# Scheduling constants of a four-layer attention kernel: second layer's row statistics on ScalarE, VectorE's share of the exponentials by every second pass, twelve query exponentials at a time

## The chip, the cores and the metric

The kernel runs on one core of one Trainium2 chip. The time is that of one execution in device microseconds, as a median of several runs; lower is better.

## The reference

A residual stream `x` of 2048 rows and 1024 columns (bf16) goes through two kinds of blocks, A, B, A, B, with the same two sets of weights each time:

```python
def layernorm(x): return (x - mean(x)) / sqrt(var(x) + 1e-5)

def A(x):      # 32 heads of 32: linear attention with a softmax feature map
    q, k, v = heads(x @ A_wqkv)
    pq, pk = q @ w_phi, k @ w_phi                     # per head
    phi_q = concat(softmax(pq), softmax(-pq))
    phi_k = concat(softmax(pk), softmax(-pk))
    o = (phi_q @ (phi_k.T @ v)) / (phi_q @ sum(phi_k) + 1e-6)
    return merge(o) @ A_wo

def B(x):      # 32 heads of 32: softmax attention
    q, k, v = heads(x @ B_wqkv)
    return merge(softmax(q @ k.T / sqrt(32)) @ v) @ B_wo

x = x + A(layernorm(x)); x = x + B(layernorm(x))
x = x + A(layernorm(x)); x = x + B(layernorm(x))
```

Each B block has 32 x 2048 x 2048 exponentials, and these are the bulk of the work.

## The kernel before

**Stages.** The text calls one A block with the B block after it a layer; there are two. Rows are worked in four chunks of 512, each of four row tiles of 128. A layer begins with A's keys and values (`a_keys`, line 768), then for each chunk come A's queries (`a_queries`, 927), its output projection into the residual `xR` (`a_out`, 1004, with the additions of line 1015), the layer normalisation of the result (`ln_rows`, 593) and B's first keys, queries and values (`b_k`, `b_q`, `b_v`, with evacuations at lines 1040 and 1041). Then comes B's attention (`attention`, 1171). While it runs, TensorE also computes the keys, values and queries of the other head groups, output projections (`b_out`, 1096) and, in the first layer, most of the next layer's A keys. Their results go through PSUM bank 7, which VectorE empties.

**The attention.** It is cut into 4096 units over both layers: a unit is the scores of one head for 128 keys and 512 queries, one PSUM bank. `group` (1215) collects up to three units, TensorE computes their scores (line 1197) into three adjacent banks, and ScalarE takes the exponentials of all three in one instruction (line 1257): a pass. Two sets of three banks, 0 to 2 and 3 to 5, are used in turn, so a pass can have its scores computed only when the pass two before it has been read. TensorE then multiplies by the values and by ones (line 1386) into bank 6, which VectorE copies out (line 1402); the denominators go through DRAM and come back spread over the rows.

VectorE takes some of the units: it reads one bank of scores (line 1339), and for two such units at a time computes the exponential with bit operations and a polynomial (`exp_dve`, lines 1147 to 1163). Its unit is chosen some units ahead of the pass at hand (`spare`, 1303; `AHEAD` units ahead). There are two ways for it. If bank 7 is free, the extra unit's scores go there (`attach`, 1346). If bank 7 was taken in the pass before, the pass may instead be made of two units for ScalarE, with the third bank of its set given to VectorE (lines 1236 to 1242):

```python
if make is after and w == WIDE and state["miss"] and n > state["mixed"] + mix(turn):
    third = spare({0, 1, 2, 3} - {u[4] for u in grp[:2]}, turn, [])
```

Here `n` counts passes, and `mix(turn)` from `MIX` says how many passes must lie between two such passes. `MOST` bounds the units that VectorE takes in a turn (one head group for one query chunk), `LOAD` the work that VectorE may have in hand when a new pair is begun, `NEAR` the distance at which a half-filled pair is closed, and `LEAD` how early its operations are due.

**Row statistics.** `ln_rows` has two ways to get the mean and variance of a row tile. With `dve` true, VectorE runs two `bn_stats` of 512 columns and a `bn_aggr` (lines 607 and 610). With it false, ScalarE makes two passes over the 1024 columns with a sum each, a copy and a square (613 and 615, each followed by a read of the accumulator), and VectorE forms the variance with two tiny operations (617 and 619). Then ScalarE takes a logarithm and an exponential (625, 628), and VectorE scales the rows (634). For chunks 0 to 2 of a B block the rows are stored to DRAM and read back transposed; for chunk 3 TensorE transposes them (644) and ScalarE copies them out (647), tile by tile. Line 1537 calls it with `LN_DVE[layer]`.

**The order of the work.** All instructions are first collected as operations with a planned duration, their dependencies, their buffers and a due time (`prio`). `Sched.run` (196) then plays the operations through and writes out one fixed order for each engine; the chip runs that order. An operation may start in the plan only when its buffers can be had: `QUOTA` bounds how many of each class are live (`eq` are the query exponentials of `a_queries`, `E` the attention's exponentials, `E1` those of VectorE, `xo` the normalised rows, `bc`, `mm`, `cmp`, `pk` and others the PSUM banks of A). The due times come from the constants in the diff: `KS`, `VS` and `VH` space keys and values of the second attention, `QL` is how early queries are due, `GAPS` and `GO` space the output projections, `PH` the steps of a chunk in A, `LA`, `LR`, `WO`, `KD`, `AW` and `BO` are leads or due times, and `SOON` and `WINDOW` bound how far ahead of the front a load may go. Where TensorE would have too little to do, the planner adds filler matmuls (1632, 1637, and idle calls of line 571 with `onesD`).

Of the kernel before, what the change touches and what calls it, by code (L numbers as in the profile page):

```python
# [60 lines left out]
class Sched:  # L61
# [52 lines left out]
    def _alloc(self, bufs):  # L114
# [19 lines left out]
        for b in new:  # L134
# [6 lines left out]
            else:  # L141
                room = sum(n for _, n in self.free)
                if b.cls in MODEST and room < b.size + RESERVE:
                    room = 0
# [51 lines left out]
    def run(self):  # L196
# [28 lines left out]
        while left:  # L225
            moved = False
            for e in engines:
# [6 lines left out]
                while ready[e] and len(skipped) < 400:  # L234
# [6 lines left out]
                    if item[3].bulk and self.wire > t + BACKLOG and self.live.get("S", 0):  # L241
                        skipped.append(item)
                        continue
                    if item[1] <= todo[front] + (SOON.get(item[3].bufs[0].cls, WINDOW) if e == "SP" and item[3].bufs and self.live.get("S", 0) else WINDOW) and not (
                            e == "PE" and self.wants is not None and item[3].bufs and item[3].bufs[0].cls == "fil"
# [99 lines left out]
SBUF_ARENA = 162 * 1024  # L345
WIDE = 3
WINDOW = 80.0
SOON = {"slabk": 24.0, "wo": 17.0, "w2": 5.0}
RESERVE = 10 * 1024
LONG = {"kT", "v", "slab", "slabk", "xn", "xn1", "kvacc", "kvm", "zm", "wnat"}  # L350
MODEST = {"slabk", "xn1", "e1", "vp1", "pkf", "wo", "bo"}
QUOTA = {"qf": 2, "qg": 6, "wqk": 1, "tl": 7, "pk": 4, "pv": 4, "kv": 4, "mm": 5, "cmp": 5, "bc": 6, "num": 1, "wt": 4, "wx": 2, "fil": 3,
         "e": 6, "vp": 6, "e1": 4, "vp1": 4, "E": 9, "q2": 2, "kt": 3, "w2": 5, "oT": 25, "T": 4, "den": 2,
         "eq": 8, "ns": 4, "cw": 6, "hl": 6, "oc": 2, "slab": 8, "slabk": 3, "fin": 4,
         "rs": 8, "pkf": 1, "cden": 2, "part": 8, "w2r": 1,
         "wo": 1, "st": 4, "xo": 9, "bn": 4, "xs": 1, "xy": 5, "xx": 1, "E1": 8}
CORE = {"E", "E1", "T", "den", "cden", "oT"}
E_SIZE = 3 * 1024
HOLES = 3
# [20 lines left out]
EACH = (False, False)  # L380
LAG = 6
KL = (17, 32)
KS = (3, 5.5)
VS = (5.0, 7.25)
WQ_AFTER = 2
BY_DVE = 2
LR = 13
LAG_X = 7
LN_DVE = (False, True)
LN_PE = (3, 3)  # L390
WO = 8
KD = 8
HALF = (False, True)
VH = 3.0
QL = (11, 12)
AW = 28
OUT_AT = (232, 256, 272)
GO = 3.0
BO = 295
PT = 2.5  # L400
QB = 18
PH = (1, 22, 44)
LA = 8
AHEAD_AT = 5
P0 = (133, 171, 244)
GAPS = (1.5, 1.5, 1.75)
PK = (142, 184, 260)
STEP = 2.5
AWAY = (-10, 12)
MIX = (lambda i: 2, lambda i: 2)  # L410
LOAD = (3.0, 2.5)
AHEAD = (36, 36)
SLACK = 11.0
NEAR = (26, 24)
LEAD = 3.0
MOST = (lambda i: 0 if i < 1 else 17, lambda i: 0 if i < 1 else 6 if i < 7 else 40)


def act_us(n):
# [15 lines left out]
def kernel(  # L435
# [81 lines left out]

    sch = Sched(ARENA, QUOTA)
    op = sch.op
# [63 lines left out]
    def load_x():  # L583
        for c in range(NC):
            for t in range(TB):
                after = row_done[4 * c + t - LAG_X:4 * c + t - LAG_X + 1] if c > 1 else ()
                xdone[c][t] = [dma(-21.0 if c == 0 else 10 * c - LR - 8, lambda c=c, t=t: nc.sync.dma_start(
                    out=xR[:, 4 * c + t, :], in_=A_x[0, c * C512 + t * P:c * C512 + (t + 1) * P, :]), after, kb=256)]
# [322 lines left out]
    def q_ahead(c, prio, xn):  # L911
        xb, xv, fin = xn
        for hf in range(2):
            at = prio + QA[hf]
            wb, ww, wd = slab("slabk", at - WO, wdq_v[:, :, hf * C512:(hf + 1) * C512], C512, [store["q"][hf]])
            for a in range(4):
# [254 lines left out]
    def attention(base, kT, vT, q_of, gate, most, mix, turns, pos, split, ahead, near, load, each):  # L1171
# [111 lines left out]
        def wants(prio):  # L1283
# [7 lines left out]
            if state["pair"] is None and (state["turn"].get(turn, 0) + 2 > most(turn)  # L1291
                                          or sch.live.get("xy", 0) >= QUOTA["xy"] or sch.live.get("E1", 0) >= QUOTA["E1"]):
                return False
# [186 lines left out]
    for layer in range(2):  # L1480
# [18 lines left out]
        for c in chunks:  # L1499
            if layer == 0:  # L1500
                next(rows_in)
                xnA[c] = ln_rows(c, 0, base + 10 * c - LR if c else -16.0, c < BY_DVE, c == 0, c == 0)
            else:
# [26 lines left out]
        for c in range(NC):  # L1530
# [3 lines left out]
            for hf in range(2):  # L1534
                a_queries(c, hf, pr + PH[0] * hf, wq_s, state, oc)
            a_out(c, pr + PH[1], wo_s, oc)
            xnB[c] = ln_rows(c, 1 + 2 * layer, pr + PH[1] + 1, LN_DVE[layer], c >= LN_PE[layer], c >= LN_PE[layer])
            b_k(0, c, pr + PH[2], wk0, kT, ANY, "ACT")
            if c == 0:
                q_of[(0, 0)] = b_q(0, 0, pr + PH[2] + 0.5, wq0, ANY)  # L1540
            for t in range(TB):
# [4 lines left out]
        for g in range(1, G):  # L1546
            pr = at + 10 * pos[(0, g)] - KL[layer]
            w = slab("w2", pr - 1, B_w[:, :, D + g * P:D + (g + 1) * P], P)
            for c in range(NC):
                b_k(g, c, pr + KS[layer] * c, w, kT, FIL, "DVE")  # L1550
        for c in range(NC):
            for t in range(TB):
                b_v(1, c, t, at + VS[layer] * (4 * c + t) + 2, bv_s[1], vT, FIL, "DVE")
                if HALF[layer]:
                    b_v(0, c, t, at + VH * (4 * c + t) + 3, bv_s[0], vT, FIL, "DVE", (1,))
        for g in range(G):
            pr = at + 10 * pos[(0, g)]
            w = slab("w2", pr - (QL[layer] + 3), B_w[:, :, g * P:(g + 1) * P], P) if g else wq0
            for qc in range(NC):
                if qc < side:  # L1560
                    if qc or g:
                        pq = at + 10 * pos[(qc, g)]
                        wq = w if pq < pr + 30 else slab("w2", pq - (QL[layer] + 3), B_w[:, :, g * P:(g + 1) * P], P)
                        q_of[(qc, g)] = b_q(g, qc, pq - QL[layer], wq, FIL)
                else:
                    away = q_away(g, qc, pr + (AW if last else AWAY[qc - 2]), w, FIL)
                    q_of[(qc, g)] = q_back(g, qc, at + 10 * pos[(qc, g)] - QB, away)
        oTs = attention(at, kT, vT, q_of, gate, MOST[layer], MIX[layer], turns, pos, SPLIT[layer], AHEAD[layer], NEAR[layer], LOAD[layer], EACH[layer])
        if last:
            bo_s = [slab("bo", at + BO + fc, B_o[:, :, fc * C512:(fc + 1) * C512], C512) for fc in range(2)]  # L1570
        new = [[[] for _ in range(TB)] for _ in range(NC)]
        for qc, p0, gap in ((0, P0[0], GAPS[0]), (1, P0[1], GAPS[1]), (2, P0[2], GAPS[2])):
            if last:
                p0, gap = OUT_AT[qc], GO
            for i in range(8):
                t, fc = (i // 2, i % 2) if last else (i % 4, i // 4)
                if not last and t == 0:
                    w = slab("wo", at + p0 + gap * i - WO, B_o[:, :, fc * C512:(fc + 1) * C512], C512)
                add = b_out(t, fc, qc, at + p0 + gap * i, bo_s[fc] if last else w, oTs[qc], FIL, last)
# [9 lines left out]
        for i in range(G):  # L1589
            pr = p0 - 7 + PT * i  # L1590
            t, fc = (i // 2, i % 2) if last else (i % 4, i // 4)
            if not last and t == 0:
                w = slab("wo", pr - WO, B_o[:, :, fc * C512:(fc + 1) * C512], C512)
            parts.append(b_out(t, fc, qc, pr, bo_s[fc] if last else w, oTs[qc], FIL, last, None, 0, 3))
# [15 lines left out]
        if not last:  # L1610

            kv = new_kv()
            for c, p0 in ((0, PK[0]), (1, PK[1]), (2, PK[2])):
                xb, xv, fin = xnA[c] = ln_rows(c, 2, at + p0, True, False, False, "xn1")
                w = [(wk_slab(at + p0 + KD + 14 * fc, fc, "slabk"), wv_slab(at + p0 + KD + 0.5 + 14 * fc, fc, cls="slabk")) for fc in range(2)]
                a_keys(c, at + p0 + KD, [w[0][0], w[1][0]], [w[0][1], w[1][1]], kv, FIL, True, STEP)
                xnA[c] = [dma(at + p0 + KD + 2, lambda c=c, xv=xv, i=i: nc.sync.dma_start(
                    out=xd_v[:, c, 2 * i:2 * i + 2, :], in_=xv()[:, 2 * i:2 * i + 2, :]), flat([fin]), [xb], kb=256, bulk=True)
# [54 lines left out]
```

## Time and profile before

| | us |
|---|---|
| median of 3 runs | 2249.85 (2249.02 to 2250.31) |
| the profiled execution | 2248.66 |
| its span, first to last instruction | 2246.9 |
| mean granted TensorE clock | 0.998 of full speed |

| part of the span | from | to |
|---|---|---|
| up to the first exponential pass | 0 | 331.83 |
| first attention | 331.83 | 1207.70 |
| between the attentions | 1207.70 | 1401.19 |
| second attention | 1401.19 | 2235.55 |
| after its last pass | 2235.55 | 2246.90 |

The profile lists for each group of instructions its line, engine and operation, the shapes, the count, busy time, the mean duration in ns, and the idle time of the engine just before them with what ended it. PE is TensorE, PEld its weight loads, DVE VectorE, ACT ScalarE, POOL GpSimd, SP SyncE. Consecutive instructions of an engine overlap in the records, so the durations of a row can add up to more than its busy time.

### The profile page before, as it was taken

How to read it: one execution, taken by the hardware profiler on the slowest of the kernel's cores; microseconds unless marked ns; L12 is line 12 of the kernel's file. 1: busy time of each engine (PE TensorE's matmuls, PEld its weight loads, DVE VectorE, ACT ScalarE, POOL GpSimd, SP SyncE). 2: the span in 40 equal slices, each digit the busy share in tenths (PEclk: the TensorE clock that was granted, in tenths of full speed). 3: DMA queues.
4: the chain of work that ended last, by engine and by line, in shares of the span. 5: the costliest groups of instructions: out<-in, count | busy, mean ns of one | idle time of the engine just before them, and what ended most of it. 6: DMA issues, size and time to landing. Idle time of an engine off the chain costs nothing.

```text
span 2246.9 us, 64847 instructions
## 1 busy us (share of the span) xinstructions
PE 2178.1 (97%) x28034; PEld 820.9 (37%) x28034; DVE 1856.5 (83%) x2630; ACT 1993.1 (89%) x1969; POOL 29.6 (1%) x78
## 2 busy tenths in 40 slices
PE   9999999999999999999999999999999999999999
PEld 5543443333333333333334444433333333333333
DVE  8866535998888999999998877376889997899997
ACT  7347669999999999999998444999999999999998
POOL 1000000000000000000000000000000000000000
PEclk9999999999999999999999999999999999999999
DMA  7821221112223423422546023111111111121111
GB/s 222 168 55 34 75 57 28 40 45 48 65 77 89 117 66 101 124 77 78 143 123 205 1 64 90 30 29 33 38 35 44 41 38 33 35 75 47 46 41 35
DMA packets 239672, 156.84 MB, mean 70 GB/s; under 512 B 131992, under 2 KB 213912, under 8 KB 239384
## 3 DMA queue, kind: packets, MB, share of 16 engines
q1 hardware_dynamic: 239384, 152.69, 25.1%
q8 instruction: 219, 3.59, 0.7%
q14 instruction: 69, 0.57, 0.1%
HBM read 85.79 MB, written 29.87 MB: 51 GB/s over the span
## 4 chain that ended last, share of the span: by engine, by line
PE 43%; ACT 41%; issue 8%; DVE 5%; DMA 2%; SPq 0%; ACTq 0%; DVEq 0%
ACT arena L1257 39%; PE psum L567 16%; PE psum L571 10%; PE psum L1386 7%; PE psum L1197 6%; PE psum L978 1%; ACT arena L788 1%; DVE work L1147 1%; PE psum L823 1%; DVE arena L1000 0%; DVE xR L1015 0%; PE psum L1632 0%; DVE arena L801 0%; PE psum L903 0%; DVE work L1339 0%
## 5 line engine op out<-in xcount | busy, mean ns | idle before, releaser
L1257 ACT ACTIVATE arena<-psum 128x1536 bf16<-128x1536 f32 (+1 forms) x1332 | 1671.7, 1433 | 9.0 <-PE psum L1197 5.2
L1386 PE MATMUL psum<-arena 128*32 128x512 bf16 x4322 | 657.6, 383 | 2.0 <-DVE arena L1402 1.4
L1386 PE MATMUL psum<-arena,ones_bf 128*32 128x512 bf16 x4322 | 657.8, 383 | 0.0
L571 PE MATMUL psum<-arena 128*32 128x512 bf16 (+1 forms) x9024 | 621.9, 376 | 6.4 <-DVE arena L801 1.5
L1197 PE MATMUL psum<-arena 32*128 32x512 bf16 x4096 | 522.3, 383 | 49.4 <-ACT arena L1257 42.6
L567 PE MATMUL psum<-arena 128*128 128x512 bf16 (+1 forms) x1968 | 434.6, 372 | 0.5
L1197 PEld LDWEIGHTS <-arena 32*128 32x128 bf16 x4096 | 154.3, 91 | 580.6 <-issue 573.0
L1339 DVE TENSOR_SCALAR work<-psum 128x512 int32<-128x512 f32 x405 | 277.3, 686 | 100.7 <-PE psum L1197 96.9
L1147 DVE SCALAR_TENSOR_TENSOR work<-work 128x1024 f32<-128x1024 f32 (+1 forms) x298 | 355.7, 1194 | 3.2
L571 PEld LDWEIGHTS <-arena 128*32 128x32 bf16 x9024 | 203.6, 95 | 256.5 <-issue 139.6
L1386 PEld LDWEIGHTS <-arena 128*32 128x32 bf16 x4322 | 186.0, 95 | 237.8 <-issue 156.4
L567 PEld LDWEIGHTS <-arena 128*128 128x128 bf16 x1968 | 185.7, 98 | 215.6 <-issue 17.6
L1147 DVE SCALAR_TENSOR_TENSOR arena<-work 128x1024 bf16<-128x1024 f32 (+1 forms) x206 | 246.4, 1196 | 2.5
L1386 PEld LDWEIGHTS <-ones_bf 128*32 128x32 bf16 x4322 | 184.4, 95 | 24.1 <-issue 4.0
L1041 DVE CAST arena<-psum 128x512 bf16<-128x512 f32 (+1 forms) x104 | 67.1, 645 | 64.3 <-PE psum L571 63.5
L788 ACT ACTIVATE arena<-psum 128x512 bf16<-128x512 f32 x80 | 43.7, 595 | 72.1 <-PE psum L567 65.9
L1402 DVE COPY arena<-psum 128x512 f32<-128x512 f32 x126 | 86.0, 682 | 6.3 <-PE psum L1386 5.0
L792 DVE TENSOR_REDUCE arena<-arena 128x32 f32<-128x1024 bf16 x64 | 77.7, 1214 | 16.1 <-ACT arena L788 15.7
L940 ACT ACTIVATE arena<-psum 128x512 bf16<-128x512 f32 x112 | 61.4, 604 | 25.8 <-PE psum L567 23.9
L801 DVE TENSOR_TENSOR arena<-psum,arena 128x1024 bf16<-128x1024 f32 x64 | 77.7, 1214 | 4.1 <-DVE arena L795 0.4
L1151 DVE TENSOR_SCALAR work<-work 128x1024 int32<-128x1024 int32 x114 | 77.6, 681 | 2.2
L1154 DVE TENSOR_SCALAR arena<-work 128x1024 uint16<-128x1024 uint16 x114 | 77.4, 679 | 0.0
(102 smaller groups left out, 1270.4 us busy)
## 6 DMA issues: line engine op xcount, KB each, us to landing
arena<-rd SPq DMA_DIRECT2D x62, 256.0 KB
arena<-in_B_wqkv_dram SPq DMA_DIRECT2D x51, 256.0 KB
xa<-arena SPq DMA_DIRECT2D x48, 256.0 KB
arena<-in_A_wqkv_dram SPq DMA_DIRECT2D x40, 256.0 KB
arena<-in_B_wo_dram SPq DMA_DIRECT2D x40, 256.0 KB
arena<-arena SPq DMA_DIRECT2D x256, 32.0 KB
arena<-wd_k SPq DMA_DIRECT2D x32, 256.0 KB
arena<-arena SPq DMA_DIRECT2D x62, 128.0 KB
```

Source lines behind the costliest of these rows:

```text
L567: nc.tensor.matmul(out_, lhsT=lhsT, rhs=rhs, start=start, stop=stop, skip_group_check=True)
L571: nc.tensor.matmul(out_[ks, :], lhsT=lhsT[:, ks], rhs=rhs, start=start, stop=stop, tile_position=(0, 32 * k), skip_group_check=True)
L792: red = op("DVE", dve_us(1024), lambda ev=ev, sv=sv: nc.vector.reduce_sum(out=sv(), in_=ev().rearrange("p s (h d) -> p (s h) d", d=DH), ax ...
L801: ml = op("DVE", dve_us(1024), lambda vpv=vpv, wv_=wv_, sv=sv: nc.vector.tensor_tensor(out=wv_()[:, :, :, 0:DH], in0=vpv().rearrange("p (h ...
L1147: return sch.later("DVE", dve_us(w * 512) + us, lambda: nc.vector.scalar_tensor_tensor(out=out_(), in0=in0(), scalar=scalar, in1=in1(), op ...
L1151: m = ts(lambda y_v=y_v, x_v=x_v: nc.vector.tensor_scalar(out=x_v().bitcast(I32), in0=y_v().bitcast(I32), scalar1=0x007FFFFF, scalar2=0x3F ...
L1154: a = ts(lambda y_v=y_v, e2_v=e2_v: nc.vector.tensor_scalar(out=e2_v().bitcast(U16), in0=high(y_v()), scalar1=0x7F80, scalar2=EXP2S_D, op0 ...
L1197: nc.tensor.matmul(out=out_, lhsT=kT[g][1]()[r, pp, d * P:(d + 1) * P], rhs=q_of[(qc, g)][1]()[r, (pp + j // 2) % 2, :], start=True, stop= ...
L1257: ex = make("ACT", act_us(w * C512), lambda: nc.scalar.activation(out=e_v()[:, 0:w * C512], in_=s_v()[:, 0:w * C512], func=ACT.Exp, scale= ...
L1339: pair["got"].append(sch.later("DVE", dve_us(512) + 0.13, lambda: nc.vector.tensor_scalar(out=y_v().bitcast(I32)[:, k, :], in0=s_v(), scal ...
L1386: nc.tensor.matmul(out=a_v()[col:col + 32, :], lhsT=v_v()[:, kc % 4, o:o + DH] if what == 0 else ones_bf[:], rhs=ev()[:, x * C512:(x + 1) ...
L1402: cp = op("DVE", dve_us(512), lambda t_v=t_v, a_v=a_v: nc.vector.tensor_copy(out=t_v(), in_=a_v()), [last], [a_b, t_b], prio - 4)
```

## The change

Only constants change. The second entry of `LN_DVE` becomes false; `MIX` goes from 2 to 1 in both layers; `eq` from 8 to 12; besides these some pool sizes, due times and the bounds on VectorE's share. What is computed stays the same.

```diff
-SOON = {"slabk": 24.0, "wo": 17.0, "w2": 5.0}
-RESERVE = 10 * 1024
+SOON = {"slabk": 24.0, "wo": 17.0, "w2": 6.0}
+RESERVE = 8 * 1024
-QUOTA = {"qf": 2, "qg": 6, "wqk": 1, "tl": 7, "pk": 4, "pv": 4, "kv": 4, "mm": 5, "cmp": 5, "bc": 6, "num": 1, "wt": 4, "wx": 2, "fil": 3,
-         "e": 6, "vp": 6, "e1": 4, "vp1": 4, "E": 9, "q2": 2, "kt": 3, "w2": 5, "oT": 25, "T": 4, "den": 2,
-         "eq": 8, "ns": 4, "cw": 6, "hl": 6, "oc": 2, "slab": 8, "slabk": 3, "fin": 4,
+QUOTA = {"qf": 2, "qg": 6, "wqk": 1, "tl": 7, "pk": 6, "pv": 4, "kv": 3, "mm": 6, "cmp": 3, "bc": 10, "num": 1, "wt": 4, "wx": 2, "fil": 5,
+         "e": 6, "vp": 6, "e1": 4, "vp1": 4, "E": 10, "q2": 2, "kt": 4, "w2": 5, "oT": 26, "T": 4, "den": 2,
+         "eq": 12, "ns": 4, "cw": 6, "hl": 6, "oc": 2, "slab": 8, "slabk": 3, "fin": 4,
          "rs": 8, "pkf": 1, "cden": 2, "part": 8, "w2r": 1,
-         "wo": 1, "st": 4, "xo": 9, "bn": 4, "xs": 1, "xy": 5, "xx": 1, "E1": 8}
+         "wo": 1, "st": 4, "xo": 10, "bn": 4, "xs": 1, "xy": 7, "xx": 1, "E1": 11}
...
-KS = (3, 5.5)
-VS = (5.0, 7.25)
+KS = (3, 6.5)
+VS = (5.0, 6.75)
...
-LR = 13
+LR = 12
 LAG_X = 7
-LN_DVE = (False, True)
+LN_DVE = (False, False)
 LN_PE = (3, 3)
-WO = 8
-KD = 8
+WO = 7
+KD = 9
 HALF = (False, True)
-VH = 3.0
-QL = (11, 12)
-AW = 28
+VH = 3.5
+QL = (11, 9)
+AW = 26
 OUT_AT = (232, 256, 272)
-GO = 3.0
-BO = 295
+GO = 2.6
+BO = 285
...
-PH = (1, 22, 44)
-LA = 8
+PH = (1, 22, 43)
+LA = 4
...
-GAPS = (1.5, 1.5, 1.75)
+GAPS = (1.5, 1.5, 2.75)
...
-MIX = (lambda i: 2, lambda i: 2)
-LOAD = (3.0, 2.5)
-AHEAD = (36, 36)
-SLACK = 11.0
-NEAR = (26, 24)
-LEAD = 3.0
-MOST = (lambda i: 0 if i < 1 else 17, lambda i: 0 if i < 1 else 6 if i < 7 else 40)
+MIX = (lambda i: 1, lambda i: 1)
+LOAD = (4.0, 3.5)
+AHEAD = (36, 42)
+SLACK = 12.0
+NEAR = (22, 24)
+LEAD = 2.0
+MOST = (lambda i: 0 if i < 1 else 15, lambda i: 0 if i < 1 else 6 if i < 7 else 40)
```

## The prediction

> **What bounds the kernel now.** I read the page's busy shares first, then the busy times of five stretches cut at the first and last exponential pass of each attention (line 1257), then that line by itself.
>
> ```profile
> span 2246.9 us, 64847 instructions
> PE 2178.1 (97%) x28034; PEld 820.9 (37%) x28034; DVE 1856.5 (83%) x2630; ACT 1993.1 (89%) x1969; POOL 29.6 (1%) x78
> PE 43%; ACT 41%; issue 8%; DVE 5%; DMA 2%; SPq 0%; ACTq 0%; DVEq 0%
> ```
>
> ```profile
> 0.00:331.83 331.83, 325.20 (x2794) 155.91 (x2795) 223.78 (x388) 197.16 (x374) 14.37 (x45) 0.99 0.41 103
> 331.83:1207.70 875.87, 840.12 (x12574) 292.34 (x12573) 785.07 (x1030) 868.91 (x729) 12.66 (x25) 1.00 0.29 83
> 1207.70:1401.19 193.49, 192.61 (x1386) 85.25 (x1386) 152.56 (x266) 97.72 (x196) 2.59 (x8) 1.00 0.30 84
> 1401.19:2235.55 834.36, 810.91 (x11239) 283.66 (x11238) 689.22 (x936) 827.86 (x670) 0.00 (x0) 1.00 0.15 39
> 2235.55:2246.90 11.35, 9.24 (x47) 3.74 (x44) 5.83 (x11) 1.48 (x5) 0.00 (x0) 1.00 0.28 94
> ```
>
> Columns of the stretches: length, then busy time of TensorE, its weight loads, VectorE, ScalarE and GpSimd, then the granted clock, the DMA share and GB/s. Over the whole span TensorE looks like the bound, but the stretches differ. In the two attentions ScalarE is busy 868.91 of 875.87 us and 827.86 of 834.36: idle only 7.0 and 6.5 us. Between them it is busy 97.72 of 193.49 us, and TensorE 192.61. So the attentions last as long as ScalarE's passes, and the stage between them as long as TensorE's matmuls.
>
> The Trainium skill ("Perfetto Trace Analysis", Identifying the Most-Contended Engine) says that a matmul busy share is no good measure, and the weight-load share is; the loads are 292.34 of 875.87 us here, which agrees. Read with TensorE as the bound, the first attention would go by its 32 added matmuls of the step below, in fours: some 1.8 us longer.
>
> ```profile
> 331.83:1207.70 875.87, 848.55 (x674) 1.00 0.29 83
> 1401.19:2235.55 834.36, 823.07 (x658) 1.00 0.15 39
> L1257 ACT ACTIVATE arena<-psum 128x1536 bf16<-128x1536 f32 x1027 | 1441.6, 1529 | 9.0 <-PE psum L1197 5.2 <-PE psum L571 1.5 <-PE psum L1386 1.0
> L1257 ACT ACTIVATE arena<-psum 128x1024 bf16<-128x1024 f32 x305 | 338.4, 1110 | 0.0
> 1411.83 18.91 ACT L1257 ACTIVATE arena<-psum 128x1536 bf16<-128x1536 f32 x14
> ```
>
> The first two rows are line 1257 alone in the attentions. A third bank adds 1529 - 1110 = 419 ns to a pass. The 1332 passes hold 3 x 1027 + 2 x 305 = 3691 banks, so of their 848.55 + 823.07 = 1671.6 us each pass has a fixed part of (1671.6 - 3691 x 0.419)/1332 = 0.094 us. In the last row, 14 three-bank passes run without a break: less the last one's 1.53, 13 steps of 1.335. If all passes ran so (two banks: 1.335 - 0.419 = 0.916), the first attention's 521 and 153 would take 835.7 us and the second's 506 and 152 814.7. With the other ScalarE work in them (868.91 - 848.55 = 20.4 and 4.8), 19.8 and 14.9 us are left: 34.7 us are lost to late scores, 0.026 a pass. That is the pool from which any better order can win.
>
> **The passes themselves.** The instruction order of the changed kernel has 1012 three-bank passes, 326 of two and two of one: 1340 for 3690 banks. VectorE takes 406 banks where it took 405. So "a third bank every second pass" changes when VectorE takes them, not how many. First attention: 674 to 677 passes, 1869 to 1866 banks: 3 x 0.094 - 3 x 0.419 = -0.98 us. Second: 658 to 663 passes, 1822 to 1824 banks: 5 x 0.094 + 2 x 0.419 = +1.31. Eight more passes at 0.026 of lateness: +0.2.
>
> The Trainium skill ("VectorE: DVE Perf Modes", the section on the TRN2 errata) gives ScalarE a fixed 172 cycles at 1.2 GHz for a read of PSUM, and so speaks against narrower passes: 0.143 us each, by estimate 0.4 us more over the eight. The rows give 0.094, which I take.
>
> **The row statistics.** Sixteen rows (four chunks of line 600's loop) go from two statistics and an aggregate on VectorE to two passes with a read of the sum on ScalarE, and two tiny VectorE subtractions.
>
> ```profile
> L607 DVE BATCH_NORM_STATS2 arena<-xR 128x6 f32<-128x512 bf16 x80 | 51.0, 675 | 1.2 <-DMA xR<-in_A_x_dram 1.2
> L610 DVE BATCH_NORM_AGGREGATE arena<-arena 128x2 f32<-128x12 f32 x40 | 8.2, 205 | 0.8
> L613 ACT ACTIVATE arena<-xR 128x1024 bf16<-128x1024 bf16 x24 | 25.3, 1056 | 23.1 <-DVE xR L1015 21.6 <-DMA xR<-in_A_x_dram 1.0 <-DVE arena L619 0.5
> L613 ACT ACTIVATION_READ_ACCUMULATOR arena<-xR 128x1 f32 x24 | 4.6, 190 | 0.0
> L619 DVE TENSOR_TENSOR arena<-arena 128x1 f32<-128x1 f32 x24 | 3.8, 158 | 6.5 <-ACT arena L615 5.6
> 240.00:330.00 90.00, 89.62 (x465) 39.47 (x462) 38.87 (x83) 57.44 (x109) 0.00 (x0) 1.00 0.31 78
> ```
>
> VectorE sheds 32 x 0.675 + 16 x 0.205 - 32 x 0.158 = 19.8 us, ScalarE gets 32 x (1.056 + 0.190) = 39.9. All lie between the attentions, where ScalarE would then be busy 138 of 193 us and TensorE still ends last. Cover for chunks 0 to 2: their rows leave by DMA and come back transposed, and the keys that read them stand some 20 planned microseconds later behind the next chunk's queries. The first layer already has it so, and in the last row, its stage with those chunks, TensorE is busy 89.62 of 90 us. Without cover, the 24 longer passes of those chunks would stand in front of query exponentials at 1.06 each, 25 us; I take 0. SyncE's queue has the same 1314 transfers in both orders; the 12 row stores start a microsecond or so later and keep their place ahead of their transposes.
>
> Chunk 3 has no such distance: its rows are transposed on TensorE and the keys follow at once.
>
> ```profile
> 1397.22 1.06 PE L644 MATMUL psum<-ident,arena 128*128 128x128 bf16 x16
> 1401.92 0.62 PE L644 MATMUL psum<-ident,arena 128*128 128x128 bf16 x8 [0.16 <-DVE arena L634]
> 1402.38 0.59 PE L1632 MATMUL psum<-xR,onesD 128*128 128x512 bf16 x2
> 1403.68 0.81 PE L1632 MATMUL psum<-xR,onesD 128*128 128x512 bf16 x3
> 1404.33 7.13 PE L567 MATMUL psum<-arena 128*128 128x256 bf16 x56
> 1411.39 0.60 PE L1197 MATMUL psum<-arena 32*128 32x512 bf16 x6
> ...
> 1397.42 0.69 DVE L1015 TENSOR_TENSOR xR<-xR,psum 128x512 bf16<-128x512 bf16 x1 [0.19 <-PE psum L567]
> ...
> 1397.87 2.99 ACT L647 COPY arena<-psum 128x1024 bf16<-128x1024 bf16 x3
> 1402.58 1.01 ACT L647 COPY arena<-psum 128x1024 bf16<-128x1024 bf16 x1
> 1408.00 0.58 ACT L1040 CAST arena<-psum 128x512 bf16<-128x512 f32 x1 [1.35 <-PE psum L567]
> 1411.49 0.37 ACT L1040 CAST arena<-psum 128x256 bf16<-128x256 f32 x1 [0.50 <-PE psum L567]
> ```
>
> The second layer before: the last row's sum is in xR at 1397.42 + 0.69 = 1398.11, its transposes (L644 x8) start at 1401.92, 3.81 us later, its copy (L647) ends at 1403.59. The same place in the first layer, with ScalarE's sums:
>
> ```profile
> 312.29 0.69 DVE L1015 TENSOR_TENSOR xR<-xR,psum 128x512 bf16<-128x512 bf16 x1 [0.21 <-PE psum L567]
> 319.91 0.61 PE L644 MATMUL psum<-ident,arena 128*128 128x128 bf16 x8
> ```
>
> There it takes 319.91 - 312.98 = 6.93 us: the second sum stands behind transposed tiles' copies in ScalarE's queue. The changed order is alike (first sum, three copies, second sum), so I take 6.93, between 3.81 (all hidden) and 9 (two more copies of 1.01 in front). The last transposes then start at 1405.04, 3.1 later. What is late next: chunk 3's keys. Before, they begin inside the group of 56 at 1404.33, behind 16 half-width matmuls of chunk 2; 8 full and 48 half ones take 7.06 us, 0.2206 a full one, so at 1406.09. After, all of chunk 2's keys and values stand ahead of the last transposes, as cover (with eight fillers of line 1632 where five were), and chunk 3's keys follow the copy, 1.67 us after the transposes: 1406.71, only 0.6 later. ScalarE, instead of idling between evacuations until 1411.86, runs five exponential passes among them where it ran one: from 1406.71, 5 x 1.335 and 0.58 + 4 x 0.37 of copies, to 1415.4. That is 3.55 us later with four passes (5.34) more behind it: -1.8. With the +1.31 of the passes, the second layer gives -0.5.
>
> **The rest.** Twelve query exponentials at a time ("eq"), other pools and due times add no instruction. TensorE's order has the same 18 fillers in the stage before the transposes above, and 32 matmuls more in the first attention (36 single fillers more, four others fewer): hidden, since a filler is put where TensorE would wait; at 0.22 a four, 1.8 us if it is not. After the last score five groups of output projection are gone, off the chain that ends the kernel (last pass, denominators, the final matmuls): 0. Keys spread over 6.5 instead of 5.5 planned microseconds, projections over 2.75 instead of 1.75, VectorE allowed a longer backlog (4 and 3.5 instead of 3 and 2.5): no row prices these. They can win at most the 34.7 us of lateness, and lose about as much if lateness doubles. A score is late where TensorE has much between two sets of scores. At 0.2206 us for a full matmul (a quarter of it for one of four that share the array), the orders of the first attention hold 39 gaps with over 1.2 us before and 38 after; those of the second 12 and 12, and with over 1.0 us 72 and 86. That is as crowded as before, so I take 0.
>
> **Sum:** -0.98 - 0.5 + 0.2 = -1.3 us. The profiled execution took 2248.66 us (its span and 1.76 around it), so 2247.4; the median of the runs, 2249.85, lies 1.2 above it, so 2248.6 for a median.
>
> **The rivals.** *Faster by less lateness.* Spread projections leave fewer places where TensorE is too full to have the next score ready. For it: 34.7 us are there to win, and VectorE gets 19.8 us freer ahead of the second attention. Against it: TensorE has no less to do, and as many crowded gaps. A third of the pool is 12 us: 2237.
>
> *Slower by crowded banks.* One mechanism, in the attentions:
>
> ```profile
> 860.00:1100.00 240.00, 227.75 (x3540) 81.25 (x3532) 229.65 (x306) 236.39 (x204) 3.38 (x8) 1.00 0.34 100
> L1147 DVE SCALAR_TENSOR_TENSOR arena<-work 128x1024 bf16<-128x1024 f32 x199 | 241.6, 1214 | 2.4
> PE psum L1197 <- ACT arena L1257: 42.6, 131, 0.9
> ```
>
> A two-bank pass leaves its third bank to VectorE, and a score that reuses those banks two passes later needs both engines done. Two-bank passes stood at least three apart (173 times exactly three), so the same banks were not taken twice running; now 141 stand two apart, always in the same three banks. VectorE is busy 229.65 of 240 us from 860 to 1100, and a conversion can stand behind an operation of 1.21 us. Scores so far wait only for ScalarE, 0.9 at most, which speaks against it. At 0.1 us for each of the 141 (an eighth of such an operation beyond what is hidden) it is +14: 2261. It decides from 0.04 each, 5.6 us.
>
> *The cover for chunk 3 fails* (9 us of wait): chunk 3 two microseconds later still, 2250.7, no change by the measure below.
>
> **How the numbers follow.** Runs of this kernel can tell 0.2% (4.5 us) from no change. The forecast, with the failed cover, has 0.40, and its own range is 2245 to 2254; less lateness has 0.33; crowded banks 0.27. The counted gaps speak for the middle, but the changed order rearranges nearly everything in both attentions and the count sees TensorE alone, so the two sides together hold more. The range for 8 in 10 runs from 2236 to 2261. Faster 0.33, same 0.40, slower 0.27.
>
> **What would show it.** Right: line 1257 with 677 and 663 passes and a busy time within 2 us of 848.55 and 823.07 in stretches cut the same way; the last row's transposes some 7 us after its sum, five passes before the last copy of line 1040; ScalarE's idle time in the attentions still near 7 us each. Wrong: mean time of a three-bank pass off 1529 by over 10 ns, TensorE waiting for VectorE at line 1197, or the stage between the attentions longer by over 8 us.

## The result, and the profile after

The changed kernel takes 2244.94 us (median of 20 runs, 2242.55 to 2247.21) against 2249.86 (20 runs, 2248.05 to 2252.06): a ratio of 0.9975, 95% interval 0.9969 to 0.9981, so 4.9 us faster. The forecast was 1.3 us and "no change". The time lies in the range, but 0.06 us below the 2245 at which the forecast's own range ends, and 0.25% is just past the 0.2% that was taken as the edge of no change (the interval reaches 0.19%). The profiled execution took 2245.84 us.

The page, then the five stretches cut as before (columns: length, busy time of TensorE, weight loads, VectorE, ScalarE and GpSimd, clock, DMA share, GB/s), then line 1257 alone in the two attentions, its forms, and two rows of the waits:

```profile
span 2244.0 us, 64781 instructions
PE 2176.6 (97%) x27992; PEld 819.0 (36%) x28053; DVE 1843.1 (82%) x2606; ACT 2025.7 (90%) x2041; POOL 30.1 (1%) x78
```

```profile
0.00:332.77 332.77, 322.67 (x2757) 156.47 (x2795) 223.79 (x388) 197.13 (x374) 14.38 (x45) 0.99 0.40 103
332.77:1206.66 873.89, 843.55 (x12602) 291.13 (x12604) 791.16 (x1028) 867.96 (x732) 13.12 (x25) 1.00 0.29 82
1206.66:1406.34 199.68, 196.70 (x1417) 89.41 (x1433) 136.70 (x252) 134.23 (x265) 2.60 (x8) 1.00 0.30 88
1406.34:2233.64 827.30, 804.77 (x11184) 278.24 (x11184) 685.67 (x929) 824.93 (x669) 0.00 (x0) 1.00 0.15 39
2233.64:2244.00 10.36, 8.91 (x42) 3.76 (x40) 5.82 (x10) 1.48 (x4) 0.00 (x0) 1.00 0.30 101
```

```profile
332.77:1206.66 873.89, 846.58 (x677) 1.00 0.29 82
1406.34:2233.64 827.30, 824.31 (x663) 1.00 0.15 39
```

```profile
L1257 ACT ACTIVATE arena<-psum 128x1536 bf16<-128x1536 f32 x1012 | 1425.0, 1529 | 5.9 <-PE psum L1197 4.2 <-issue 0.3 <-PE psum L571 0.3
L1257 ACT ACTIVATE arena<-psum 128x1024 bf16<-128x1024 f32 x326 | 361.9, 1110 | 1.3 <-PE psum L1197 1.1
```

```profile
PE psum L1197 <- ACT arena L1257: 40.5, 119, 0.9
PE psum L1197 <- DMA arena<-arena: 1.4, 1, 1.4
```

The passes are those counted beforehand, 677 and 663, at the same 1529 and 1110 ns. The score sets still wait for ScalarE, 0.9 us at most, and once, 1.4 us, for a DMA. The first attention is 2.0 us shorter, the end 1.0. The stage between the attentions is 6.2 longer and the second attention 7.1 shorter, which are two sides of one thing, since five passes now run while the last keys and values are made. So it is better to cut there at the end of the last key and value copy (line 1040). The second and third part by that cut, before and after:

```profile
1207.72:1411.87 204.15, 203.13 (x1470) 92.55 (x1469) 153.10 (x267) 103.96 (x209) 2.59 (x8) 1.00 0.30 84
1411.87:2235.55 823.68, 800.39 (x11155) 276.36 (x11154) 688.67 (x935) 821.59 (x657) 0.00 (x0) 1.00 0.15 39
```

```profile
1206.66:1414.82 208.16, 204.92 (x1488) 93.80 (x1503) 136.70 (x252) 142.71 (x276) 2.60 (x8) 1.00 0.30 86
1414.82:2233.64 818.82, 796.55 (x11116) 273.85 (x11114) 685.67 (x929) 816.45 (x658) 0.00 (x0) 1.00 0.15 39
```

+4.0 up to that copy and -4.9 after it. All kernels below are compared by these parts: first attention, from its end to the last copy, from there to the end of the last pass, and the rest. "Late" is worked out as in the prediction: the length of the first attention, less its passes at 1.335, 0.916 and (one bank) 0.497 us, less the other ScalarE work in it. "Late after the copy" is the same for the passes behind the last copy; there is no other ScalarE work there.

### The profile page after: what moved, and what is told of

It is laid out like the page before. It is cut to its first block, busy times and chain, and to the rows that moved or that the text cites. A ratio compares the mean times of both kernels' runs of the same rounds, so it can differ in the third digit from the quotient of the medians.

```text
span 2244.0 us, 64781 instructions
## 1 busy us (share of the span) xinstructions
PE 2176.6 (97%) x27992; PEld 819.0 (36%) x28053; DVE 1843.1 (82%) x2606; ACT 2025.7 (90%) x2041; POOL 30.1 (1%) x78
## 4 chain that ended last, share of the span: by engine, by line
PE 31%; ACT 24%; issue 5%; DVE 2%; DMA 1%; SPq 0%; ACTq 0%; DVEq 0%
ACT arena L1257 22%; PE psum L571 9%; PE psum L1386 8%; PE psum L1197 6%; PE psum L567 6%; ACT arena L788 1%; PE psum L978 0%; PE psum L1632 0%; DMA arena<-arena 0%; DVE work L1339 0%; DVE work L1147 0%; PE psum L903 0%; DMA arena<-in_B_wqkv_dram 0%; DVE arena L1147 0%; DVE arena L1000 0%
## 5 line engine op out<-in xcount | busy, mean ns | idle before, releaser
L567 PE MATMUL psum<-arena 128*128 128x512 bf16 (+1 forms) x1914 | 428.4, 372 | 5.1 <-issue 2.1
L1147 DVE SCALAR_TENSOR_TENSOR work<-work 128x1024 f32<-128x1024 f32 x295 | 357.4, 1211 | 2.6
L1147 DVE SCALAR_TENSOR_TENSOR arena<-work 128x1024 bf16<-128x1024 f32 x204 | 246.8, 1210 | 2.7
L792 DVE TENSOR_REDUCE arena<-arena 128x32 f32<-128x1024 bf16 x64 | 77.7, 1215 | 17.8 <-ACT arena L788 17.3
L613 ACT ACTIVATE arena<-xR 128x1024 bf16<-128x1024 bf16 x40 | 42.2, 1056 | 46.1 <-DVE xR L1015 44.1
L1151 DVE TENSOR_SCALAR work<-work 128x1024 int32<-128x1024 int32 (+1 forms) x113 | 77.2, 683 | 2.3
```

Of the source, the lines that this page charges most:

```text
L567: nc.tensor.matmul(out_, lhsT=lhsT, rhs=rhs, start=start, stop=stop, skip_group_check=True)
L792: red = op("DVE", dve_us(1024), lambda ev=ev, sv=sv: nc.vector.reduce_sum(out=sv(), in_=ev().rearrange("p s (h d) -> p (s h) d", d=DH), ax ...
L1147: return sch.later("DVE", dve_us(w * 512) + us, lambda: nc.vector.scalar_tensor_tensor(out=out_(), in0=in0(), scalar=scalar, in1=in1(), op ...
L1151: m = ts(lambda y_v=y_v, x_v=x_v: nc.vector.tensor_scalar(out=x_v().bitcast(I32), in0=y_v().bitcast(I32), scalar1=0x007FFFFF, scalar2=0x3F ...
```

## The experiments

| kernel | ratio to before (95%) | first attention | late | to the last copy (passes ahead of it) | after it | late after the copy | rest |
|---|---|---|---|---|---|---|---|
| before | 1 | 875.9 | 19.9 | 204.1 (1) | 823.7 | 10.3 | 11.35 |
| before_again | 1.0000 (0.9991 to 1.0009) | 876.3 | 20.2 | 204.2 (1) | 823.3 | 10.0 | 11.34 |
| b_ln | 1.0012 (1.0003 to 1.0021) | 877.2 | 20.9 | 208.0 (1) | 823.6 | 11.4 | 10.4 |
| b_gaps | 1.0003 (0.9993 to 1.0012) | 876.4 | 20.4 | 204.4 (1) | 825.3 | 11.5 | 10.2 |
| b_vec | 0.9983 (0.9974 to 0.9993) | 876.0 | 20.0 | 200.4 (1) | 825.1 | 12.1 | 10.3 |
| changed | 0.9975 (0.9969 to 0.9981) | 873.9 | 17.8 | 208.2 (5) | 818.8 | 9.8 | 10.4 |
| after_again | 0.9974 (0.9965 to 0.9984) | 872.7 | 16.5 | 209.0 (5) | 818.8 | 9.8 | 10.4 |
| a_ln | 0.9985 (0.9976 to 0.9993) | 872.2 | 16.1 | 202.6 (0) | 824.9 | 12.9 | 10.5 |
| a_eq | 0.9984 (0.9974 to 0.9993) | 876.3 | 19.9 | 208.8 (5) | 819.2 | 10.5 | 10.3 |
| a_mixB | 0.9999 (0.9989 to 1.0008) | 874.2 | 18.3 | 208.2 (5) | 822.3 | 11.7 | 10.5 |
| a_gaps | 0.9976 (0.9967 to 0.9986) | 875.3 | 19.4 | 207.1 (5) | 819.6 | 11.4 | 10.5 |
| a_mixA | 0.9986 (0.9976 to 0.9995) | 876.1 | 20.1 | 203.9 (5) | 819.3 | 10.2 | 11.1 |
| a_vec | 1.0001 (0.9992 to 1.0011) | 877.6 | 21.5 | 204.2 (5) | 823.3 | 13.8 | 10.6 |
| a_three | 0.9995 (0.9986 to 1.0004) | 879.6 | 23.3 | 199.3 (0) | 826.0 | 10.3 | 11.2 |

Lengths in us, one profiled execution each; the ratios are of 9 to 20 runs of each kernel beside 20 or 31 of the kernel before, whose median moved between 2249.4 and 2251.1 from one such group of runs to another. Kernels whose names begin with b start from the kernel before, those with a from the changed one. The expectations speak of two theories: by the passes theory only the counted passes change, by the lateness theory less time is lost to late scores.

### The same kernels again

No edit.

> The kernel before once more, to see how far one profiled execution of the same instructions differs from another, stage by stage. Both theories: total within 2 us of 2249.9. If the stage up to the first exponential pass moves by about 1 us while the attentions stay within 1 us of 875.9 and 834.4, the 0.9 us that the changed kernel's profile shows in that first stage is chance, and the profiled pair understates the gain. If the stage after the last pass is 10.4 instead of 11.35, its 1.0 us was chance too.

> The changed kernel once more. Passes theory (the sum of the prediction, -1.3 us, with lateness unchanged): the time lies by chance at the low end and a second sample goes to about 2248.6. Lateness theory (less time lost to late scores, as in its first profile with 17.8 and 10.7 us against 19.8 and 14.9): again 2245, with the attentions within 1 us of 873.9 and 827.3.

Measured: 2249.38 and 2243.12 us. The changed kernel's gain is no accident of its first runs. The stage up to the first pass was 331.8 and 333.0 in two executions of the same instructions, so the 0.9 us by which the changed kernel's profile is longer there (332.8, then 332.5) is chance. The first attentions moved by 0.4 and 1.2 us, and the 1.0 at the end came again.

### The row statistics alone

```diff
-LN_DVE = (False, True)
+LN_DVE = (False, False)
```

> The kernel before with the second layer's row statistics on ScalarE and nothing else. Its first attention has the same passes, its second 659 passes of 1819 banks (-1.2 us by the prices of the prediction). In its order an exponential pass stands in front of the last row's logarithm, so the last transposes come 8.3 us after the row's sum instead of 6.9, and only one pass runs before the last key and value copy: +2.0. Passes theory: 2250.6, no change to be measured. If the row statistics on ScalarE are what makes the changed kernel faster: 2246 or less.

Measured: 1.0012, some 3 us slower than before; its first attention is the same order as before, instruction by instruction. The loss is where it was expected, but 3.9 us instead of 2.0. Timelines of VectorE, TensorE and ScalarE, then two stretches with the columns of above:

```profile
1400.14 0.69 DVE L1015 TENSOR_TENSOR xR<-xR,psum 128x512 bf16<-128x512 bf16 x1 [0.21 <-PE psum L567]
...
1408.07 0.61 PE L644 MATMUL psum<-ident,arena 128*128 128x128 bf16 x8 [2.50 <-ACT arena L1040]
1408.52 8.59 PE L567 MATMUL psum<-arena 128*128 128x256 bf16 x54
...
1405.40 1.46 ACT L1257 ACTIVATE arena<-psum 128x1536 bf16<-128x1536 f32 x1
...
1417.14 0.37 ACT L1040 CAST arena<-psum 128x256 bf16<-128x256 f32 x1 [0.50 <-PE psum L567]
```

```profile
1405.84:1409.25 3.41, 1.18 (x15) 1.21 (x16) 0.55 (x1) 2.96 (x7) 0.00 (x0) 1.00 0.10 20
1409.25:1412.66 3.41, 3.41 (x14) 1.83 (x13) 0.00 (x0) 1.13 (x3) 0.00 (x0) 0.50 0.44 101
```

The last row is complete at 1400.83 and its transposes start at 1408.07: 7.2 us, with 2.5 of them TensorE standing still. The exponential pass is queued on ScalarE ahead of the row's logarithm, and no more than this one pass runs in the wait, as before. Here the cover for chunk 3 fails, which the prediction had priced as a rival for the changed kernel. Most of the excess over 2.0 us is the clock: in this execution it is granted at 0.50 for 3.41 us right behind TensorE's wait, and the 54 matmuls of the keys take 8.59 us, where the 56 before took 7.13.

The other way round, in the changed kernel:

```diff
-LN_DVE = (False, False)
+LN_DVE = (False, True)
```

> The changed kernel with the second layer's row statistics back on VectorE. 677 passes of 1866 banks, then 661 of 1815 (-1.0 and -2.7 us against before); no pass runs ahead of the last key and value copy, which should come at about 1410 us (-0.3). Passes theory: 2246, some 2.5 us below what it gives for the changed kernel. If the row statistics on ScalarE are what makes the changed kernel faster: 2249 or more.

Measured: 0.9985 (2245.57 us). That is the passes theory's 2246, but not for its reason: it had a_ln 2.5 us below the changed kernel, and a_ln came out 0.6 and 2.4 us above the changed kernel's two medians. The number fits because the changed kernel itself is faster than that theory has it. The first attention is in the same order as the changed kernel's. Its parts against the changed kernel's:

```profile
332.22:1204.42 872.20, 843.45 (x12600) 291.22 (x12602) 791.01 (x1028) 867.80 (x732) 12.04 (x25) 1.00 0.29 82
1204.42:1407.02 202.60, 201.34 (x1475) 92.72 (x1467) 153.75 (x268) 102.69 (x208) 2.60 (x8) 1.00 0.31 89
1407.02:2231.94 824.92, 800.81 (x11204) 276.47 (x11203) 703.96 (x954) 820.60 (x662) 0.00 (x0) 1.00 0.15 39
```

The last copy comes 6.0 us earlier than the changed kernel's mean of 208.6, and the time after it is 6.1 us longer. Of these, 3.0 are passes, since all 661 are then still to come. The other 3.1 are lateness: late after the copy is 12.9 us here and 9.8 in the changed kernel. By the profiles the statistics on ScalarE and the five passes in their wait come out even in the changed kernel only because of this second part, whose cause stays open.

### VectorE's bounds in the first attention

Into the kernel before (b_vec), and out of the changed one (a_vec, the same lines the other way):

```diff
-MIX = (lambda i: 2, lambda i: 2)
-LOAD = (3.0, 2.5)
-SLACK = 11.0
-NEAR = (26, 24)
-LEAD = 3.0
-MOST = (lambda i: 0 if i < 1 else 17, lambda i: 0 if i < 1 else 6 if i < 7 else 40)
+MIX = (lambda i: 1, lambda i: 2)
+LOAD = (4.0, 2.5)
+SLACK = 12.0
+NEAR = (22, 24)
+LEAD = 2.0
+MOST = (lambda i: 0 if i < 1 else 15, lambda i: 0 if i < 1 else 6 if i < 7 else 40)
```

> The kernel before with the changed kernel's bounds on VectorE's share in the first attention (a third bank every second pass, MOST 15, LOAD 4, NEAR 22, and LEAD 2, SLACK 12 in both). First attention 676 passes of 1867 banks, second 659 of 1821. Passes theory: first attention 875.5 (-0.7), in all 2248.5. If these bounds are what lowers the lateness of the first attention: it lasts about 873.3, as in the changed kernel, and lateness among its banks 1080 to 1620 falls from 8.0 us to about 3.4; in all 2246.

> The changed kernel with the bounds of before on VectorE's share in the first attention. 676 passes of 1869 banks there, 663 of 1825 in the second. Passes theory: first attention 874.5 (1.2 above the changed kernel's 873.3), in all 2246. If these bounds lower the lateness: first attention 876 and lateness among banks 1080 to 1620 back near 8 us, in all 2248.

By the totals both look like the lateness theory: 0.9983 with the bounds and 1.0001 without. By the parts neither is. In a_vec the first attention is 4.3 us longer than the changed kernel's mean of 873.3, as that theory had it, but 4.4 us come back up to the last copy. What its total loses lies after the copy, 823.3 us instead of 818.8 with the same number of passes: 13.8 us late there instead of 9.8. `SLACK` and `LEAD` act on both attentions, and a_mixA below, which leaves them alone, has 819.3 after the same first attention; neither was tried by itself. b_vec is faster in a place that no theory had named, its first attention not at all:

```profile
332.44:1208.44 876.00, 845.97 (x12635) 293.05 (x12637) 789.83 (x1028) 868.97 (x732) 12.16 (x25) 1.00 0.30 84
1208.44:1408.88 200.44, 197.33 (x1409) 91.10 (x1423) 152.03 (x266) 104.56 (x208) 2.60 (x8) 1.00 0.28 78
```

200.4 us to the last copy instead of 204.2. What goes with it is how much of the last output projection the planner had left over when the first attention ended. Counted in the orders, the fours of line 571 that still stand behind the last scores are 26 before, 28 in the changed kernel, 24 in a_gaps, 19 in b_vec, and 18 in a_vec, a_mixA and a_three, with 18, 18, 9, 13 and 13 fillers (line 571's idle fours apart: one before, seven in a_gaps). With five passes ahead of the copy, 28, 24 and 18 left over go with 208.6, 207.1 and 204.1 us; with one, 26 and 19 with 204.2 and 200.4. This was counted and not varied by itself. The changed kernel gains nothing here, its order being as poor as before's.

### Spread projections

```diff
-GAPS = (1.5, 1.5, 1.75)
+GAPS = (1.5, 1.5, 2.75)
```

> The kernel before with the third query chunk's output projections in the first attention spread over 2.75 instead of 1.75 planned microseconds each, and nothing else. Same 674 passes of 1869 banks there. Passes theory: first attention 876, in all 2249.5. If the spread projections lower the lateness: banks 1440 to 1620, where they stand, fall from 3.4 us to about 1.5 and the first attention lasts 874; in all 2247.5.

> The changed kernel with these projections back at 1.75. 676 passes of 1866 banks in the first attention, 662 of 1822 in the second. Passes theory: first attention 873.3, in all 2243.5. If the spread lowers the lateness: banks 1440 to 1620 rise from 1.5 to about 3.4 us and the first attention lasts 875; in all 2246.

Measured: 1.0003 and 0.9976, so neither moves the total. But b_gaps doesn't test the theory: its first attention came out in the same order as before, instruction by instruction. In a_gaps the order did change, late time went from 17.8 and 16.5 to 19.4, and the projections left over fell from 28 to 24, so it comes to about the same. Of the 19.4, a part is the clock: it is at half for 6.8 us in this first attention, for 3.4 in the changed kernel's.

### The third bank, by attention

```diff
-MIX = (lambda i: 1, lambda i: 1)
+MIX = (lambda i: 2, lambda i: 1)
```

> The changed kernel with the third bank at every third pass again in the first attention only. 676 passes of 1869 banks there, 663 of 1824 in the second; between the attentions it has 13 fillers and 18 groups of projections where the changed kernel has 18 and 28, as a_vec has, which took 4.4 us less there. If the spacing of third banks alone carries the lateness of a_vec: first attention 877.6, in all 2245.5. If it does not (passes theory): first attention 874.5, in all 2242.4, the fastest so far.

```diff
-MIX = (lambda i: 1, lambda i: 1)
+MIX = (lambda i: 1, lambda i: 2)
```

> The changed kernel with the third bank at every third pass again in the second attention only. Same first attention (873) and same stage up to the last key and value copy (208.6); second attention 657 passes of 1829 banks instead of 663 of 1824: 1.5 us more by the prices. Passes theory: 2246.5 to 2247.3. If closer third banks crowd the second attention: 2244 or less.

a_mixA: 0.9986. Its first attention is the same order as a_vec's, instruction by instruction, so of all bounds in a_vec only the third bank's spacing touched it.

```profile
332.95:1209.09 876.14, 840.08 (x12560) 291.81 (x12562) 784.80 (x1026) 868.99 (x732) 12.39 (x25) 1.00 0.29 84
1209.09:1413.01 203.92, 202.51 (x1462) 92.10 (x1450) 134.93 (x250) 143.13 (x277) 2.60 (x8) 1.00 0.27 77
```

This order took 877.6, 876.1 and 879.6 us in three kernels (a_vec, a_mixA, a_three), the changed kernel's 873.9, 872.7, 872.2, 874.2 and 876.3 in five (itself twice, a_ln, a_mixB, a_eq), and the order of before 875.9, 876.3, 877.2 and 876.4 in four. The means are 877.8, 873.8 and 876.5. The spacing is worth 4.0 us of the first attention in the changed kernel, and 4.5 us are lost again up to the last copy, where more projections are left over. Much of the scatter within an order goes with the granted clock (last section): with one half-clock stretch each, the three orders took 877.6, 872.2 to 873.9, and 876.3 and 877.2. The expected 2245.5 lies between its runs (2246.5) and its profile (2245.14).

a_mixB: 0.9999, 2249.31 us, 2 us above what either theory gave. 822.3 us after the last copy instead of 818.8: 1.5 of the 3.5 are five banks more on ScalarE less six passes' fixed part, the rest is lateness. In this order closer third banks don't crowd the second attention, they help it. The spacing alone in the kernel before wasn't tried.

### Eight query exponentials, and all three named parts undone

```diff
-         "eq": 12, "ns": 4, "cw": 6, "hl": 6, "oc": 2, "slab": 8, "slabk": 3, "fin": 4,
+         "eq": 8, "ns": 4, "cw": 6, "hl": 6, "oc": 2, "slab": 8, "slabk": 3, "fin": 4,
```

> The changed kernel with eight query exponentials out at a time instead of twelve. Same first attention and same order up to the second attention, 663 passes of 1823 banks there. Both theories: as the changed kernel within 1 us, 2244.5 to 2245.5, since the query exponentials stand where TensorE ends last.

Measured: 2245.86 us (0.9984), 0.4 above the expected range and 0.9 and 2.7 above the changed kernel's two medians; the intervals of the ratios overlap, so a small loss is neither shown nor excluded. Its profiled execution, at 2250.02 us the slowest of its ten, shows 876.3 for a first attention whose order is the changed kernel's, with the clock at half for 10.2 us of it.

```diff
-         "eq": 12, "ns": 4, "cw": 6, "hl": 6, "oc": 2, "slab": 8, "slabk": 3, "fin": 4,
+         "eq": 8, "ns": 4, "cw": 6, "hl": 6, "oc": 2, "slab": 8, "slabk": 3, "fin": 4,
-LN_DVE = (False, False)
+LN_DVE = (False, True)
-MIX = (lambda i: 1, lambda i: 1)
+MIX = (lambda i: 2, lambda i: 2)
```

> The changed kernel with all three parts that its short description names undone: statistics on VectorE, a third bank every third pass, eight query exponentials; the other constants stay. 676 passes of 1869 banks, then 659 of 1824, no pass ahead of the last key and value copy, 13 fillers between the attentions. If the first attention is as a_vec's, 877.6: 2247.7. If it is 874.5: 2244.6, and the other constants alone give the gain.

Measured: 2249.01 us (0.9995). The first attention is not the 874.5 of the passes theory but 879.6. The other constants alone don't give the gain.

## Why the prediction was right or wrong

The range held and the sign came out right, but the sum holds only 1.3 of the 4.9 us. The counted parts were sound; most of the gain lies in two terms that were put at about nothing, so that the time fell into the range owes something to its width.

**What bounds the kernel: right.** ScalarE is idle 5.9 and 2.4 us in the attentions after (6.96 and 6.5 before), and what the attentions won or lost was a later or earlier pass. Only the second of these idle times isn't "near 7": before, 4.5 us of it lay between the first pass and the last copy, after, 0.9, as the passes now run there.

**The passes: right.** 677 and 663 of 1866 and 1824 banks at unchanged prices. The prices themselves were a little off. The row of 14 passes gives a step of 1.337 and not 1.335, and by the starts of passes with nothing between them the steps are 1.330 or 1.331 and 0.904 in both kernels (0.916 was taken). A bank is then 0.426 and the fixed part 0.05, where the mean durations had given 0.419 and 0.094. The two terms become -1.1 and +1.1, and late time 4.4 to 4.5 us more in the first attention of either kernel, so no comparison changes.

**The row statistics: right, nearly to the step.** Timelines of VectorE, TensorE and ScalarE of the changed kernel:

```profile
1396.92 0.69 DVE L1015 TENSOR_TENSOR xR<-xR,psum 128x512 bf16<-128x512 bf16 x1 [0.21 <-PE psum L567]
...
1404.57 0.61 PE L644 MATMUL psum<-ident,arena 128*128 128x128 bf16 x8
...
1406.56 1.46 PE L567 MATMUL psum<-arena 128*128 128x512 bf16 x6 [0.33 <-ACT arena L647]
...
1398.70 2.96 ACT L647 COPY arena<-psum 128x1024 bf16<-128x1024 bf16 x3
...
1406.34 2.86 ACT L1257 ACTIVATE arena<-psum 128x1536 bf16<-128x1536 f32 x2
...
1414.29 0.53 ACT L1040 CAST arena<-psum 128x256 bf16<-128x256 f32 x1
```

The last row is complete at 1397.61 and its transposes start at 1404.57: 6.96 us, taken as 6.93 from the first layer. The keys follow at 1406.56 (1406.71), the last copy ends at 1414.82 (1415.4), five passes ahead of it. That the times themselves agree is in part luck, since the first attention ended 1.0 us earlier than the one before: counted from its end, the keys came 0.9 us later than forecast, the last copy 0.5 (1.3 in the second execution). Over two executions each, the part up to that copy is 4.4 us longer and the part after it 4.7 shorter: -0.3 for the second layer where -0.5 stood. The row of the trace was worth more than the arithmetic: the same step in another stage gave the wait, the queue ahead of it included.

**Lateness: the term that was mis-sized.** It was put at +0.2, by eight more passes, because the count of crowded TensorE gaps was the same in both orders. In the first attention it fell from 20.0 to 17.2 us over two executions each. With the other ScalarE work there 1.1 us more, -0.98 became -2.8 in all. How a late pass comes about was right, as an example from before shows, TensorE's rows first:

```profile
1056.79 0.39 PE L1197 MATMUL psum<-arena 32*128 32x512 bf16 x3
...
1057.98 1.04 PE L571 MATMUL psum<-arena 128*32 128x512 bf16 x16
1058.95 0.61 PE L1197 MATMUL psum<-arena 32*128 32x512 bf16 x6
...
1053.58 5.24 ACT L1257 ACTIVATE arena<-psum 128x1536 bf16<-128x1536 f32 x4
1059.48 3.71 ACT L1257 ACTIVATE arena<-psum 128x1536 bf16<-128x1536 f32 x3 [0.65 <-PE psum L1197]
```

Two score sets are 2.16 us apart with no pause between their matmuls; a pass lasts 1.335, and ScalarE stands 0.65. From the starts in the traces, passes over 0.1 us late, those behind other ScalarE work left out, number 87 before (22.0 us in both attentions), and in 78 of them TensorE had no pause of 0.15 us between the two sets; after, 91 (22.2 us) and 88. By attention these are 13.4 us before and 12.2 after in the first, 8.7 and 9.9 in the second. What fell clearly is TensorE's waiting for VectorE in the first attention, at lines other than 1197. Counted in waits over 0.15 us it was 14 times and 5.2 us before (13 and 4.8 in the second execution), the longest at line 801, in the next layer's A keys:

```profile
PE psum L571 <- DVE arena L801: 1.5, 3, 1.1
```

After, it was 8 times and 2.2 us in both executions. That is as much as the lateness fell; but b_vec, with 2.9 us of such waits, is 20.0 us late, so it is not shown that they carry the gain. A count of crowded gaps in TensorE's order sees neither these waits nor where a gap falls against ScalarE's passes.

**The rival "crowded banks": wrong in its sign.** With 141 two-bank passes two apart, the first attention became faster, and a_mixA and a_mixB show that wider spacing costs 4.0 us there and some 2 us of lateness in the second. The spacing was not tried alone from the kernel before, where b_vec, with closer banks among other bounds, shows no gain in the first attention. TensorE never waited for VectorE at line 1197. (The price of 0.1 us was a twelfth of 1.21 us, not an eighth.)

**The rival "less lateness": right in direction**, at 2.8 us for the first attention, not 12, and not by its reason: the spread of projections did not carry it, the third banks did, in the one order in which they were tried alone.

**The end: 0 was wrong, it is -1.0.** VectorE's last additions, before and after:

```profile
2243.04 1.28 DVE L1110 TENSOR_TENSOR arena<-arena,psum 128x512 bf16<-128x512 f32 x2 [1.01 <-DMA out_dram<-arena]
```

```profile
2238.97 2.48 DVE L1110 TENSOR_TENSOR arena<-arena,psum 128x512 bf16<-128x512 f32 x4 [0.27 <-PE psum L567]
```

Before, the last two wait 1.01 us for a store to free its buffer, after, none does. The wait stood in the trace, and the prediction did not look there. No one edit carries it, as b_ln, b_gaps and b_vec lost it too (10.2 to 10.4 us).

Together, over two executions each: +0.2 up to the first pass, -2.8, +4.4, -4.7 and -0.95, in all -3.8 us. The medians differ by 4.9 and, in the second sample, 6.3. A part of what is missing goes with the clock. The four executions are not alike in it: in the first attention the kernel before has no half-clock stretch in one and one in the other, the changed kernel one in each. Compared with one stretch each, the first attention gains 3.8 us and not 2.8 (876.3 and 877.2, of before_again and b_ln, against 873.9, 872.7 and, in a_ln, 872.2). And in the second sample 8 of the 9 runs of the changed kernel had a mean clock of 0.998 (2243.8 us on average), of before 17 of 31 (2248.8): 5.0 us at the same clock.

## What to carry to other kernels

Where one engine is full for hundreds of microseconds, first count its instructions in the new order and price them; what is left over is lateness, and its sum comes only from running the order. For a step that moves to another engine, look in the trace for the same step already done that way: its wait, taken whole, was right to 0.03 us here. Compare variants by stages and not by totals: b_vec and a_vec told one story in their totals and another in their parts.

## What the runs showed of the hardware

Lateness repeats: two executions of the kernel before gave 19.9 and 20.2 us in the first attention and, from the first pass on, lengths of its parts equal to 0.4 us. The changed kernel's order of the first attention scattered more, 872.2 to 876.3 us in five executions of the same instructions, so one profile does not settle 2 us there.

That scatter goes with the granted clock. In the traces it is 1 or, for one or a few stretches of 3.41 us, 0.5; a matmul of line 1386 then takes 0.61 to 0.63 us instead of 0.38. Within one order the first attention lengthens with the number of such stretches in it: 872.2, 872.7 and 873.9 with one, 874.2 with two, 876.3 with three in the changed kernel's order; 876.1, 877.6 and 879.6 with none, one and two in a_mixA's; 875.9 and 876.4 with none, 876.3 and 877.2 with one in that of before. The clock falls only where TensorE has been waiting:

```profile
1151.53:1154.94 3.41, 1.55 (x62) 0.83 (x63) 1.54 (x3) 3.39 (x5) 0.00 (x0) 1.00 0.02 6
1154.94:1158.35 3.41, 3.41 (x35) 0.87 (x27) 3.38 (x5) 2.14 (x2) 0.00 (x0) 0.50 0.03 6
```

These are two neighbouring stretches of a_eq, TensorE busy 1.55 us of the first. Cut into such stretches, in step with the clock's changes and from 100 us on, the 14 traces have 8606 at full clock with TensorE busy 70% or more, and none of them is followed by half clock; of the 82 with less, 19 are. So a wait of TensorE can cost twice, as in b_ln between the attentions.

A ScalarE pass with a sum is followed by a separate read of the accumulator of 0.19 us, of which 0.1 overlaps the pass (1.06 us, the read starting 0.96 after the pass).
